# Capped attention and a spatial gating unit on one core: outputs issued by ScalarE, denominators as 28 rows of 32, v in two loads, a new order

## The chip, the cores and the metric

The kernel runs on one core of a Trainium2 chip. The metric is the device time of one execution in microseconds (us); shown is the median of 3 runs. PE is TensorE, DVE is VectorE, ACT is ScalarE, POOL is GpSimd, SP is SyncE, which in this kernel before the change issues every DMA.

## The reference

```python
# q, k, v: (8, 12, 448, 64)
scores = cap * tanh(q @ k.T / 8 / cap)
scores = scores - max(scores, axis=-1)
attn = exp(scores)
attn = attn / (sum(attn, axis=-1) + 1e-9)
x = (attn @ v)                      # heads put side by side: (8, 448, 768)
h = maximum(x @ w_in, 0)            # (8, 448, 1024), halves u and v
v_n = (v - mean(v)) / sqrt(var(v) + 1e-6)
v_s = w_spatial @ v_n + b_spatial   # over the 448 positions
out = (u * v_s) @ w_out             # (8, 448, 768)
```

cap is 30, w_in and w_out arrive as 64-bit floats.

## The kernel before

**Attention.** The 12 heads of a batch are worked in 3 quads of four heads, 24 quads in all (`quad_bnd`, called once per quad; `turn` counts them). Scores are computed transposed, keys on partitions: for each of the 7 blocks of 64 keys, four float32 products of 64 x 64 x 448 fill one PSUM tile of 128 x 896 (L584, task `sc`). ACT takes tanh (L588) and, for two blocks at a time, exp (L595). PE multiplies the exponentials by v (L605, task `pv`). Since the cap bounds the scores, exp is taken without subtracting the maximum; DVE finds the maximum of the exponentials (the reference's epsilon is scaled by it) and their sum by folding the tiles on each other (L623), a 32 x 32 block transpose (L631) and a reduction (L633), which leaves 28 columns for each of two partition halves. For the first three quads (`PE_SUMS = 3`) PE computes the sums with a matrix of ones (L651), ACT copies them out (L660), and they go through DRAM twice to get into the layout of the maxima: `td<-u` (L664), then `dt<-td` (L667).

**Denominators.** In `dt`, partition i holds one of 32 positions and the 28 columns the blocks of 32 queries, so positions lie block by block down the columns. DVE makes the denominator (L673) and its reciprocal (L675). Two DMAs write it to DRAM (`rd<-dt`, L676), two more spread it over the partitions of each head (`rr<-rd`, L680). DVE multiplies the attention output by it (L690, task `xmul`); rr is read there with a step of 14 elements. ACT and DVE then split the product into two parts whose sum carries float32 (L345 `xg<-xf`, L341 `xg<-xf`).

**The second part** (`moe`, once per batch; here "the FF block"): products with w_in (L743 to L745 for u, L765 to L770 for v), layer norm on DVE, ACT and POOL, products with w_spatial (L834 to L839), the gate (L844), products with w_out (L859 to L861), six copies out of PSUM per batch by ACT (L345 `o<-ps_acc`) and six stores by SP (L865, `out<-o`). Each product is three one-pass products of split operands. The weights are split at the start (L403 to L417, L341, L345).

**Order.** Every instruction is a task with an engine, an assumed length, a key and dependences. `Plan.order` simulates the engines with these lengths and takes, among the tasks that can start, the one with the smallest key; the keys come from the tables `BND_KEY`, `BND_ADJ`, `BND_W_KEYS`. Each engine, and SP's DMA queue, then works its list in that order. PE changes between its two ways of tiling (64-row products of attention, 128-row products of the FF block) when the list changes over; `STICK` is the planner's reluctance to do so. xg has 7 buffers, o 2, PSUM has two tiles each for `s` and `acc` and one for `x`.

```python
add("S", HW, k, lambda o=o, ns=ns: nc.sync.dma_start(out=out[b, ns, :], in_=o.t), [r], [o], lat=XF * 128 * S)
x, r = x.rearrange("p (b i) -> p b i", i=32), r.rearrange("p (i b) -> p b i", b=QB)
```

Of the kernel before, what the change touches and what calls it, by code (L numbers as in the profile page):

```python
# [9 lines left out]
F32 = mybir.dt.float32  # L10
# [32 lines left out]
class Plan:  # L43
# [8 lines left out]
    TURN, STICK = 180.0, 2.7208  # L52
# [31 lines left out]
    def order(self):  # L84
# [35 lines left out]
        while done < len(self.tasks):  # L120
# [24 lines left out]
            while again:  # L145
                again = False
                for e in ["A", *("VP" if holder == "V" else "PV"), "S", "T"]:
# [20 lines left out]
                    if e == "S":  # L168
                        dma = max(dma, took.end + 650.0) + took.lat
                        took.lat = dma + 1000.0 - took.end  # L170
# [13 lines left out]
HW, HH, XL, XF = 475, 650, 50, 4 / 360  # L184
# [24 lines left out]
def gpc(n):  # L209
# [21 lines left out]
    "v": (4 * D, F32, 4), "tp": (2 * PW, F32, 6),  # L231
    "xf": (PW, F32, 2), "rr": (PW, F32, 2), "st": (64, F32, 2), **MOE_TAGS, "xg": (XW, F32R, 7),
# [6 lines left out]
BND_KEY = dict(ld=15.1316, vld=10.6595, sc=-4.3972, th=0.8221, ex=-13.3346, pv=2.8747, sm=5.6221, mx=2.7207,  # L239
               dn=-3.5316, ev=-2.5342, x=1.255, moe=3.3159, span=11.7552, step=-1.2625, mv=-7.4324, vld_=0.4935, sc_=0.475,  # L240
               th_=0.213, ex_=2.8729, pv_=0.0973, sm_=0.5533, mx_=0.887)
BND_ADJ = dict(sc0=1.8257, sc1=1.698, sc2=0.6056, sc3=3.487, sc4=2.4891, sc5=0.9848, sc6=1.9465, sc7=1.2566,
               sc8=-0.2027, sc9=-0.0525, sc10=-1.0199, sc11=-1.6861, sc21=0.372, sc22=0.2759, sc23=-0.0304, mx0=4.147, mx1=2.3102,
               mx2=-1.5569, mx3=-2.5816, mx4=-1.7021, mx5=-3.8682, mx6=-3.7708, mx7=-2.1194, mx8=2.2658, mx9=6.0412, mx10=4.2055,
               mx11=1.3621, mx21=-0.5191, mx22=-1.2175, mx23=5.0057, sm0=1.8357, sm1=-4.3389, sm2=0.1127, sm3=-1.9888,
               sm4=-3.2252, sm5=-6.4566, sm6=-4.1062, sm7=-2.4598, sm8=-0.1718, sm9=4.6664, sm10=2.3463, sm11=0.4051,
               sm21=-1.2777, sm22=-3.1044, sm23=2.1372, dn0=-6.9641, dn1=1.8515, dn2=-0.9662, dn3=3.7809, dn4=8.6087, dn5=5.0673,
               dn6=1.1656, dn7=-2.366, dn8=0.4341, dn9=2.5001, dn10=4.9471, dn11=-4.3505, dn21=14.2648, dn22=10.8391, dn23=8.4438,
               x0=-1.2869, x1=-4.0561, x2=-5.6099, x3=-5.4773, x4=2.351, x5=0.6484, x6=4.0904, x7=0.1021, x8=2.4533, x9=6.1666,
               x10=4.3613, x11=1.3018, x21=-0.0656, x22=-3.6008, x23=0.1225, moe0=-0.4749, moe1=-0.3715, moe2=-0.6357,  # L250
               moe3=-0.003, moe7=-4.8205, span0=0.237, span1=0.5291, span2=-5.1693, span3=-3.6031, span7=51.1417, mv0=3.2517,
               mv1=1.1849, mv2=5.0071, mv3=5.7847, mv7=-5.1134, wi0=-11.8899, wi1=-7.682, wi2=-25.3033, wi3=9.6125, wi4=12.6292,
               wi5=4.2564, wi6=0.1225, wi7=-1.8938, wi8=-6.6204, wi9=0.3494, wi10=-1.8774, wi11=-9.6153, ws0=-12.9749, ws1=4.598,
               ws2=-15.4035, ws3=-9.2649, wo0=-5.5216, wo1=-4.7934, wo2=-5.3784, wo3=1.0364)
# [12 lines left out]
def attn_moe(ctx, tc, bounded, shared, qk, v, qk2, v2, cap, w_in, w_sp, w_out, out):  # L267
# [95 lines left out]
    def split_f32(key, c):  # L363
# [27 lines left out]
    def split_f64(key, src, hi, lo, n, late=False):  # L391
# [11 lines left out]
        t = add("S", HW, key, lambda: nc.sync.dma_start(out=w.t.bitcast(U32)[:, :2 * n], in_=src), allocs=[w], lat=XF * 256 * n)  # L403
# [39 lines left out]
    def v_any(b, hp, key):  # L443
# [3 lines left out]
        a = add("S", HW, key - 1, lambda: nc.sync.dma_start(out=r.t, in_=v[b, hp]), allocs=[r], lat=XF * 128 * 512)  # L447
# [4 lines left out]
    def head_any(b, h, vt, vdep, xf, rr, after):  # L452
# [9 lines left out]
        t0 = add("S", 2 * HW, k - 2.0, ld, allocs=[raw], lat=XF * 128 * 896)  # L462
# [42 lines left out]
        def den():  # L505
# [8 lines left out]
                   [rr] if e == 0 else [], lat=XF * D * S)  # L514
# [40 lines left out]
    def quad_bnd(b, n):  # L555
# [5 lines left out]
        for c in range(2):  # L561
# [15 lines left out]
        for i in range(NB):
# [39 lines left out]
        sec = lambda i: dt.t[:96, i * n1:(i + 1) * n1]  # L617
        done = []
        for a, op, key in ((0, ALU.max, "mx"), (1, ALU.add, "sm"))[:1 if by_pe else 2]:
            r = Buf("red")  # L620

            def fold(o_, i0, i1, op=op):
# [11 lines left out]
                out=st.t[:, a * n1:(a + 1) * n1], in_=blk(r1()), axis=AX.X), [d, *done], [r, st], [st] if a == 0 else [], name="red3"))  # L634
        d = done
        for c in range(2):
            p = slice(2 * c * 32, (2 * c + 1) * 32)
            o = slice((2 * c + 1) * 32, (2 * c + 2) * 32)
            d = [add("A", 145, kk("dn"), lambda p=p, o=o: nc.scalar.copy(out=sh.t[p, :n1 * len(done)], in_=st.t[o, :n1 * len(done)]), d,
                     [st, sh], [sh] if c == 0 else [], name="shift")]  # L640
        d = add("V", 106, kk("dn"), lambda: nc.vector.tensor_tensor(sec(0), st.t[:96, :n1], sh.t[:96, :n1], op=ALU.max), d,
                [st, sh, dt], [dt], name="mred2")
        if by_pe:
            accs, sxs, td = [Buf("acc"), Buf("acc")], [Buf("u"), Buf("u")], Buf("td")
# [14 lines left out]
            for c in range(2):  # L659
                q = add("A", act(S) + 420, kk("ev"), lambda c=c: nc.scalar.copy(  # L660
                    out=sxs[c].t.rearrange("p (i b) -> p b i", b=QB), in_=accs[c].t[:, 0, :S].rearrange("p (b i) -> p b i", i=32)), [s],
                    [accs[c], sxs[c]], [sxs[c]], name="sev")
                for e in range(2):
                    outs.append(add("S", HW, kk("dn"), lambda c=c, e=e: nc.sync.dma_start(  # L664
                        out=td.t[(2 * c + e) * S:(2 * c + e + 1) * S], in_=sxs[c].t[D * e:D * e + 1]), [q], [sxs[c], td],
                        [] if outs else [td], lat=XL))
            d1 = [d] + [add("S", HW, kk("dn"), lambda c=c: nc.sync.dma_start(  # L667
                out=dt.t[2 * c * 32:(2 * c + 1) * 32, 2 * n1:3 * n1].rearrange("p (e b) -> p e b", b=QB),
                in_=td.t[2 * c * S:2 * (c + 1) * S].rearrange("(e p b) -> p e b", e=2, b=QB)), [d, *outs], [td, dt], lat=XL) for c in range(2)]
        else:  # L670
            d1 = [add("V", 106, kk("dn"), lambda: nc.vector.tensor_tensor(sec(1), st.t[:96, n1:2 * n1], sh.t[:96, n1:2 * n1], op=ALU.add), [d],
# [272 lines left out]
```

## Time and profile before

| | |
|---|---|
| median of 3 runs | 735.85 us (735.57 to 736.28) |
| the profiled execution | 735.29 us |
| its span, first to last instruction | 733.5 us |
| mean granted clock of TensorE | 0.994 of full |
| PE busy | 716.0 us (98%) |
| DVE busy | 609.6 us (83%) |
| ACT busy | 481.4 us (66%) |
| POOL busy | 79.0 us (11%) |
| DMA | 66.52 MB, mean 91 GB/s |

A busy row of PE is the union of its matmuls, whose ends are modelled, so it holds both work and slow stretches. The row of a line tells how many instructions it had, the busy time of all, the mean of one in ns, and the idle time of the engine just before them with what ended it.

### The profile page before, as it was taken

How to read it: one execution, taken by the hardware profiler on the slowest of the kernel's cores; microseconds unless marked ns; L12 is line 12 of the kernel's file. 1: busy time of each engine (PE TensorE's matmuls, PEld its weight loads, DVE VectorE, ACT ScalarE, POOL GpSimd, SP SyncE). 2: the span in 40 equal slices, each digit the busy share in tenths (PEclk: the TensorE clock that was granted, in tenths of full speed). 3: DMA queues.
4: the chain of work that ended last, by engine and by line, in shares of the span. 5: the costliest groups of instructions: out<-in, count | busy, mean ns of one | idle time of the engine just before them, and what ended most of it. 6: DMA issues, size and time to landing. Idle time of an engine off the chain costs nothing.

```text
span 733.5 us, 12340 instructions
## 1 busy us (share of the span) xinstructions
PE 716.0 (98%) x4902; PEld 485.3 (66%) x4902; DVE 609.6 (83%) x825; ACT 481.4 (66%) x648; POOL 79.0 (11%) x69
## 2 busy tenths in 40 slices
PE   8997999999999999999999999999999999999997
PEld 2333675574587586955778557767659576679896
DVE  4999999999999998949999299989899598884620
ACT  6999865858856957388573794867773865833421
POOL 1353011500100002000210003000020001000100
PEclk9998999999999999999999999999999999999999
DMA  7556232533212432052230431214311321002002
GB/s 268 192 192 200 67 111 63 164 102 107 90 32 85 143 100 76 1 150 82 72 102 11 140 103 33 69 44 160 101 47 56 101 76 51 26 26 88 14 2 80
DMA packets 43167, 66.52 MB, mean 91 GB/s; under 512 B 8782, under 2 KB 33884, under 8 KB 43100
## 3 DMA queue, kind: packets, MB, share of 16 engines
q1 hardware_dynamic: 43100, 65.64, 28.3%
q8 instruction: 40, 0.66, 0.4%
q14 instruction: 27, 0.22, 0.1%
HBM read 54.42 MB, written 11.20 MB: 89 GB/s over the span
## 4 chain that ended last, share of the span: by engine, by line
PE 63%; DVE 21%; ACT 6%; DMA 5%; issue 3%; SPq 1%; POOL 0%; DVEq 0%; ACTq 0%
PE ps_s L584 10%; PE ps_x L605 9%; DVE red L623 8%; PE ps_acc L859 4%; PE ps_acc L860 4%; PE ps_acc L861 4%; PE ps_acc L743 4%; PE ps_acc L744 4%; PE ps_acc L745 4%; DMA rr<-rd 3%; PE ps_acc L768 2%; PE ps_acc L770 2%; PE ps_acc L769 2%; ACT tp L595 2%; PE ps_acc L837 2%
## 5 line engine op out<-in xcount | busy, mean ns | idle before, releaser
L588 ACT ACTIVATE tp<-ps_s,capt 128x896 f32<-128x896 f32 x168 | 162.3, 1005 | 19.7 <-PE ps_s L584 13.7
L595 ACT ACTIVATE tp<-tp,capt 128x1792 f32<-128x1792 f32 x96 | 154.3, 1609 | 1.5
L623 DVE TENSOR_TENSOR red<-red,tp 128x1792 f32<-128x1792 f32 x90 | 140.0, 1555 | 14.7 <-ACT tp L595 13.2
L584 PE MATMUL ps_s<-raw 64*64 64x448 f32 x1344 | 147.1, 544 | 3.0 <-ACT tp L588 2.7
L605 PE MATMUL ps_x<-tp,v 64*64 64x448 f32 x1344 | 140.6, 537 | 2.0 <-ACT tp L595 1.7
L623 DVE TENSOR_TENSOR red<-tp 128x1792 f32<-128x1792 f32 x45 | 90.9, 2021 | 24.1 <-ACT tp L595 23.1
L605 PEld LDWEIGHTS ps_x<-tp,v 64*64 64x64 f32 x1344 | 50.4, 133 | 78.2 <-issue 67.8
L584 PEld LDWEIGHTS ps_s<-raw 64*64 64x64 f32 x1344 | 46.2, 132 | 80.4 <-issue 43.8
L792 POOL TENSOR_TENSOR lst<-lst,capt 128x1 f32<-128x1 f32 x32 | 38.6, 1208 | 521.8 <-DVE lst L790 521.8
L743 PE MATMUL ps_acc<-xg,wi_h 128*128 128x448 f32 x180 | 67.7, 376 | 3.2 <-ACT xg L345 3.2
L744 PE MATMUL ps_acc<-xg,wi_h 128*128 128x448 f32 x180 | 66.1, 367 | 1.2 <-DVE xg L341 1.2
L745 PE MATMUL ps_acc<-xg,wi_l 128*128 128x448 f32 x180 | 66.1, 367 | 0.0
L859 PE MATMUL ps_acc<-xg,wo_h 128*128 128x448 f32 x176 | 65.2, 371 | 0.4 <-DVE o L844 0.3
L860 PE MATMUL ps_acc<-xg,wo_h 128*128 128x448 f32 x176 | 64.0, 364 | 0.5 <-DVE xg L341 0.5
L861 PE MATMUL ps_acc<-xg,wo_l 128*128 128x448 f32 x176 | 63.6, 361 | 0.0
L690 DVE TENSOR_TENSOR xf<-xf,rr 128x448 f32<-128x448 f32 x48 | 44.4, 951 | 20.8 <-DMA rr<-rd 20.8
L345 ACT CAST xg<-o 128x448 fp32r<-128x448 f32 x32 | 17.9, 566 | 61.5 <-DVE o L844 53.5
L623 DVE TENSOR_TENSOR red<-red 128x896 f32<-128x896 f32 x45 | 50.6, 1123 | 0.5
L631 DVE STREAM_TRANSPOSE red<-red 128x896 f32<-128x896 f32 x45 | 49.6, 1103 | 0.5
L768 PE MATMUL ps_acc<-wi_h,xg 128*128 128x512 f32 x126 | 50.0, 397 | 0.0
L633 DVE TENSOR_REDUCE st<-red 128x28 f32<-128x896 f32 x45 | 48.6, 1079 | 0.8
L769 PE MATMUL ps_acc<-wi_l,xg 128*128 128x512 f32 x126 | 49.1, 390 | 0.0
(141 smaller groups left out, 1121.0 us busy)
## 6 DMA issues: line engine op xcount, KB each, us to landing
raw<-in_qk SPq DMA_DIRECT2D x48, 448.0 KB
rr<-rd SPq DMA_DIRECT2D x48, 224.0 KB
out<-o SPq DMA_DIRECT2D x48, 224.0 KB
v<-in_v SPq DMA_DIRECT2D x72, 128.0 KB
w<-in_w_in SPq DMA_DIRECT2D x12, 512.0 KB
xg<-in_w_out SPq DMA_DIRECT2D x12, 256.0 KB
v<-in_v SPq DMA_DIRECT2D x24, 64.0 KB
rd<-dt SPq DMA_DIRECT2D x48, 3.5 KB
```

The source lines that it names most:

```text
L584: nc.tensor.matmul(ps.t[c * D:(c + 1) * D, e, :S], lhsT=f(raw[c].t)[r, k:k + D], rhs=f(raw[c].t)[r, :S], start=True, stop=True)
L588: th = add("A", act(PW, 1), kk("th", i), lambda ps=ps, tp=tp, o=o: nc.scalar.activation(out=tp.t[:, o:o + PW].rearrange("p (e q) -> p e q" ...
L595: ex = add("A", act_s(w, 1), kk("ex", i), lambda tp=tp, w=w: nc.scalar.activation(out=tp.t[:, :w], in_=tp.t[:, :w], func=AF.Exp, scale=ca) ...
L605: nc.tensor.matmul(x.t[e * D:(e + 1) * D, c, :S], lhsT=vts[g].t[c * D:(c + 1) * D, (2 * j + e) * D:(2 * j + e + 1) * D], rhs=tp.t[c * D:(c ...
L623: nc.vector.tensor_tensor(o_(), i0(), i1(), op=op)
L743: nc.tensor.matmul(ps, lhsT=wi1_h[:, c, fs], rhs=x[:, XH:], start=(c == 0), stop=False)
L744: nc.tensor.matmul(ps, lhsT=wi1_h[:, c, fs], rhs=x[:, :S], start=False, stop=False)
L745: nc.tensor.matmul(ps, lhsT=wi1_l[:, c, fs], rhs=x[:, XH:], start=False, stop=(c == NP - 1))
L768: nc.tensor.matmul(ps, lhsT=x[:, XH:][:, ts], rhs=wi2_h[:, c], start=(c == 0), stop=False)
L859: nc.tensor.matmul(ps, lhsT=wo_h[:, c, ns], rhs=g[:, XH:], start=(c == 0), stop=False)
L860: nc.tensor.matmul(ps, lhsT=wo_h[:, c, ns], rhs=g[:, :S], start=False, stop=False)
L861: nc.tensor.matmul(ps, lhsT=wo_l[:, c, ns], rhs=g[:, XH:], start=False, stop=(c == 3))
```

## The change

- The six stores of a batch are issued by ACT (`nc.scalar.dma_start`), right behind the copies in ACT's own list, in place of SP.
- Maxima and sums stay in `st` in sections of 32 columns, of which 28 are used. A block transpose on DVE (task `dtr`, one per quad) turns them into 28 rows of 32, so that a row holds 32 queries that follow each other. `rd<-dt` moves 28 rows of 32 elements in place of 32 x 2 runs of 14, and rr comes out in the order of xf: the multiply reads both without a step.
- The sums of the first three quads are copied out of PSUM without a rearrangement and go straight from `u` into `dt` by DMA; the trip through `td` is gone.
- v of a quad is loaded in two pieces (128 x 512 and 128 x 384) into two buffers, in place of four pieces into four; the memory is the same.
- The planner's assumed lengths for DMAs change, and all keys are new, so the order of all engines is new.

```diff
-            add("S", HW, k, lambda o=o, ns=ns: nc.sync.dma_start(out=out[b, ns, :], in_=o.t), [r], [o], lat=XF * 128 * S)
+            add("A", 340, kv(k), lambda o=o, ns=ns: nc.scalar.dma_start(out=out[b, ns, :], in_=o.t), [r], [o], lat=2500, name="odma")
...
-    "v": (4 * D, F32, 4), "tp": (2 * PW, F32, 6),
-    "xf": (PW, F32, 2), "rr": (PW, F32, 2), "st": (64, F32, 2), **MOE_TAGS, "xg": (XW, F32R, 7),
+    "v": (8 * D, F32, 2), "tp": (2 * PW, F32, 6),
+    "xf": (PW, F32, 2), "rr": (PW, F32, 2), **MOE_TAGS, "xg": (XW, F32R, 7),
...
-        for g in range(4):
-            w = min(4 * D, PW - 4 * D * g)
+        for g in range(2):
+            w = min(8 * D, PW - 8 * D * g)
...
-                q = add("A", act(S) + 420, kk("ev"), lambda c=c: nc.scalar.copy(
-                    out=sxs[c].t.rearrange("p (i b) -> p b i", b=QB), in_=accs[c].t[:, 0, :S].rearrange("p (b i) -> p b i", i=32)), [s],
+                q = add("A", act(S), kk("ev"), lambda c=c: nc.scalar.copy(out=sxs[c].t, in_=accs[c].t[:, 0, :S]), [s],
                     [accs[c], sxs[c]], [sxs[c]], name="sev")
                 for e in range(2):
                     outs.append(add("S", HW, kk("dn"), lambda c=c, e=e: nc.sync.dma_start(
-                        out=td.t[(2 * c + e) * S:(2 * c + e + 1) * S], in_=sxs[c].t[D * e:D * e + 1]), [q], [sxs[c], td],
-                        [] if outs else [td], lat=XL))
-            d1 = [d] + [add("S", HW, kk("dn"), lambda c=c: nc.sync.dma_start(
-                out=dt.t[2 * c * 32:(2 * c + 1) * 32, 2 * n1:3 * n1].rearrange("p (e b) -> p e b", b=QB),
-                in_=td.t[2 * c * S:2 * (c + 1) * S].rearrange("(e p b) -> p e b", e=2, b=QB)), [d, *outs], [td, dt], lat=XL) for c in range(2)]
+                        out=dt.t[64 * c + e * QB:64 * c + (e + 1) * QB, 32:64],
+                        in_=sxs[c].t[D * e:D * e + 1].rearrange("p (b i) -> p b i", i=32)), [q, room], [sxs[c], dt], lat=dm(QB, 128)))
+            d = [add("V", 106, kk("dn"), lambda: nc.vector.transpose(out=sec(dt, 0), in_=sec(st, 0)), [d, room], [st, dt], name="dtr"), *outs]
...
+            d = [add("V", 140, kk("dn"), lambda: nc.vector.transpose(out=dt.t[:96, :64].rearrange("p (a i) -> p a i", i=32),
+                in_=st.t[:96, :64].rearrange("p (a i) -> p a i", i=32)), [d, room], [st, dt], name="dtr")]
...
-            out=rd.t[2 * c * S:2 * (c + 1) * S].rearrange("(e p b) -> p e b", e=2, b=QB),
-            in_=dt.t[2 * c * 32:(2 * c + 1) * 32, :n1].rearrange("p (e b) -> p e b", b=QB)), [d], [dt, rd], [] if c else [rd], lat=XL)
+            out=rd.t[c * PW:(c + 1) * PW].rearrange("(p i) -> p i", i=32), in_=dt.t[64 * c:64 * c + n1, 32:64]), [d], [dt, rd], [] if c else [rd],
+            lat=dm(n1, 128)) for c in range(2)]
...
-                x, r = x.rearrange("p (b i) -> p b i", i=32), r.rearrange("p (i b) -> p b i", b=QB)
                 eng[E_X[0]].tensor_tensor(x, x, r, op=ALU.mult)
...
-BND_KEY = dict(ld=15.1316, vld=10.6595, sc=-4.3972, th=0.8221, ex=-13.3346, pv=2.8747, sm=5.6221, mx=2.7207,
+BND_KEY = dict(ld=21.3368, vld=21.4975, sc=-5.2844, th=0.946, ex=-11.0691, pv=4.9062, sm=6.2433, mx=2.4129,
```

What the new keys do to the lists is shown at three places; in the new kernel lines L584, L743, L690, L341, L345 and L865 are L592, L749, L696, L349, L353 and L871.

PE's list at the first products of the FF block, before (`raw` is q and k, `xg` the split attention output, `wi_h` and `wi_l` the parts of w_in):

```order
L584 MATMUL ps_s<-raw_158 64x448 x2
L743 MATMUL ps_acc<-xg,wi_h 128x448
L744 MATMUL ps_acc<-xg,wi_h 128x448
L745 MATMUL ps_acc<-xg,wi_l 128x448
L743 MATMUL ps_acc<-xg,wi_h 128x448
L744 MATMUL ps_acc<-xg,wi_h 128x448
L745 MATMUL ps_acc<-xg,wi_l 128x448
L584 MATMUL ps_s<-raw_157 64x448 x2
L584 MATMUL ps_s<-raw_158 64x448 x2
L584 MATMUL ps_s<-raw_157 64x448 x2
L584 MATMUL ps_s<-raw_158 64x448 x2
L743 MATMUL ps_acc<-xg,wi_h 128x448
```

And now:

```order
L592 MATMUL ps_s<-raw_61 64x448 x2
L749 MATMUL ps_acc<-xg,wi_h 128x448
L750 MATMUL ps_acc<-xg,wi_h 128x448
L751 MATMUL ps_acc<-xg,wi_l 128x448
L749 MATMUL ps_acc<-xg,wi_h 128x448
L750 MATMUL ps_acc<-xg,wi_h 128x448
L751 MATMUL ps_acc<-xg,wi_l 128x448
L592 MATMUL ps_s<-raw_60 64x448 x2
L592 MATMUL ps_s<-raw_61 64x448 x2
L749 MATMUL ps_acc<-xg,wi_h 128x448
```

Ahead of the first six products stand 68 groups of four 64-row products before and 71 now; between them and the next products stand two groups before and one now.

DVE's list at the same place (`xf<-xf,rr` is the multiply by the reciprocal, `xg<-xf,xg` the second part of the split, `wy` and `wi_l` the splitting of w_in), before:

```order
L690 TENSOR_TENSOR xf<-xf,rr 128x448 x2
L341 TENSOR_TENSOR wi_l<-wy,wi_h 128x512
L341 TENSOR_TENSOR xg<-xf,xg 128x448 x3
L641 TENSOR_TENSOR dt_172<-st,sh_164 96x28
L414 TENSOR_SCALAR wy<-wy 128x512
```

And now:

```order
L696 TENSOR_TENSOR xf<-xf,rr 128x448 x2
L422 TENSOR_SCALAR wy<-wy 128x512 x2
L349 TENSOR_TENSOR xg<-xf,xg 128x448 x2
L423 SCALAR_TENSOR_TENSOR wy<-w_649,wy 128x512
L349 TENSOR_TENSOR xg<-xf,xg 128x448
L425 SCALAR_TENSOR_TENSOR wy<-w_649,wy 128x512
L349 TENSOR_TENSOR xg<-xf,xg 128x448
L650 TENSOR_TENSOR st_165<-st_165,sh_161 96x28
```

Before, one of the four splits of the first two quads stands earlier in the list, behind the first quad's multiply, and three stand here; now all four stand here, behind the second quad's multiply.

ACT's list at the first stores, before (`o<-ps_acc` is the copy out of PSUM, `tp<-ps_s` tanh, `tp<-tp` exp):

```order
L345 COPY o<-ps_acc 128x448 x3
L588 ACTIVATE tp<-ps_s,capt 128x896 x2
L345 COPY o<-ps_acc 128x448
L595 ACTIVATE tp<-tp,capt 128x1792
L345 COPY o<-ps_acc 128x448
```

And now:

```order
L353 COPY o<-ps_acc 128x448
L871 DMA out<-o 128x448
L353 COPY o<-ps_acc 128x448
L871 DMA out<-o 128x448
L353 COPY o<-ps_acc 128x448
L871 DMA out<-o 128x448
L596 ACTIVATE tp<-ps_s,capt 128x896 x2
L353 COPY o<-ps_acc 128x448
L603 ACTIVATE tp<-tp,capt 128x1792
L871 DMA out<-o 128x448
```

Each copy now has its store behind it in ACT's list; of the 48 stores 26 have another copy of this kind next, and 4 have a tanh next.

## Rows read from the trace of the kernel before

**Rows 1.** The page's busy times and slices of PE, and the granted clock.

```profile
PE 716.0 (98%) x4902; PEld 485.3 (66%) x4902; DVE 609.6 (83%) x825; ACT 481.4 (66%) x648; POOL 79.0 (11%) x69
...
PE   8997999999999999999999999999999999999997
...
PEclk9998999999999999999999999999999999999999
```

**Rows 2.** What PE waited for: us in total, times, longest.

```profile
PE ps_acc L743 <- ACT xg L345: 3.2, 1, 3.2
PE ps_s L584 <- ACT tp L588: 2.7, 7, 0.7
PE ps_x L605 <- ACT tp L595: 1.7, 3, 0.8
...
PE ps_acc L744 <- DVE xg L341: 1.2, 1, 1.2
PE ps_acc L651 <- POOL wy L410: 0.9, 1, 0.9
PE ps_acc L860 <- DVE xg L341: 0.5, 1, 0.5
PE ps_x L605 <- ACT xf L611: 0.3, 1, 0.3
PE ps_acc L859 <- DVE o L844: 0.3, 1, 0.3
```

**Rows 3.** The chain that ended last, 60 to 75 us: start, us, what.

```profile
60.64 1.49 DMA rd<-dt
...
62.82 5.15 DMA rr<-rd
...
67.99 1.77 DVE xf L690 x2
...
70.36 1.52 DVE xg L341 x2
```

**Rows 4.** Timeline of PE, 55 to 80 us: start, us, line, count, idle before.

```profile
65.00 1.85 PE L584 MATMUL ps_s<-raw 64*64 64x448 f32 x16
70.03 0.74 PE L743 MATMUL ps_acc<-xg,wi_h 128*128 128x448 f32 x1 [3.18 <-ACT xg L345]
71.93 0.74 PE L744 MATMUL ps_acc<-xg,wi_h 128*128 128x448 f32 x1 [1.16 <-DVE xg L341]
```

**Rows 5.** Windows: PE, PEld, DVE, ACT, POOL busy, PEclk, DMA share, GB/s.

```profile
65.00:70.00 5.00, 1.85 (x17) 0.41 (x16) 4.04 (x5) 4.06 (x6) 1.15 (x2) 0.96 0.88 232
70.00:75.00 5.00, 3.81 (x9) 3.08 (x10) 5.00 (x8) 4.92 (x10) 0.95 (x1) 0.50 0.33 120
75.00:80.00 5.00, 5.00 (x38) 3.15 (x41) 5.00 (x8) 3.74 (x5) 0.00 (x0) 0.86 0.08 10
```

**Rows 6.** Groups by form: busy us, mean ns, idle before and its releasers.

```profile
L690 DVE TENSOR_TENSOR xf<-xf,rr 128x448 f32<-128x448 f32 x48 | 44.4, 951 | 20.8 <-DMA rr<-rd 20.8
L341 DVE TENSOR_TENSOR xg<-xf,xg 128x448 fp32r<-128x448 f32 x48 | 28.9, 631 | 3.5 <-ACT xg L345 3.5
...
L641 DVE TENSOR_TENSOR dt<-st,sh 96x28 f32<-96x28 f32 x24 | 4.2, 179 | 2.7 <-ACT sh L639 2.6
```

**Rows 7.** Groups by form: the copies of ACT.

```profile
L345 ACT COPY o<-ps_acc 128x448 f32<-128x448 f32 x44 | 23.5, 535 | 30.0 <-PE ps_acc L861 25.9 <-DVE red L623 2.1 <-ACT xg L345 1.0
...
L660 ACT COPY u<-ps_acc 128x448 f32<-128x448 f32 x6 | 5.2, 984 | 0.0
```

**Rows 8.** Line L865 on SP's queue: ns min/median/max, first and last start.

```profile
L865 SPq DMA_DIRECT2D out<-o x48: 332/338/585, 155.0 to 729.0; - x48
```

**Rows 9.** What SP's queue waited for: us in total, times, longest.

```profile
SPq L865 <- ACT o L345: 92.6, 33, 36.8
SPq L865 <- ACT sh L639: 54.8, 4, 24.0
```

**Rows 10.** Timeline of the last 8.5 us, the last copy out of PSUM.

```profile
728.41 0.53 ACT L345 COPY o<-ps_x 128x448 f32<-128x448 f32 x1 [1.87 <-PE ps_x L861]
```

More of the change, by code (lines that the diff above doesn't have):

```diff
@@ L169, in order @@
                         dma = max(dma, took.end + 650.0) + took.lat
-                        took.lat = dma + 1000.0 - took.end
+                        took.lat = dma + 900.0 + 0.55 * took.lat - took.end
                     busy[e] = took.end
@@ L183, with dm @@
 FF = 751
-HW, HH, XL, XF = 475, 650, 50, 4 / 360
+HW, HH, XL = 400, 620, 50
+def dm(packets, size):
+    return packets * (4.0 + 0.0016 * size)
 def act(n, extra=0):
@@ L633, in quad_bnd @@
             done.append(add("V", dve(PW), kk(key, 5), lambda r1=r1, a=a, red=red: red(
-                out=st.t[:, a * n1:(a + 1) * n1], in_=blk(r1()), axis=AX.X), [d, *done], [r, st], [st] if a == 0 else [], name="red3"))
+                out=st.t[:, a * 32:a * 32 + n1], in_=blk(r1()), axis=AX.X), [d, *done], [r, st], [st] if a == 0 else [], name="red3"))
         d = done
@@ L638, in quad_bnd @@
             o = slice((2 * c + 1) * 32, (2 * c + 2) * 32)
-            d = [add("A", 145, kk("dn"), lambda p=p, o=o: nc.scalar.copy(out=sh.t[p, :n1 * len(done)], in_=st.t[o, :n1 * len(done)]), d,
+            d = [add("A", 145, kk("dn"), lambda p=p, o=o: nc.scalar.copy(out=sh.t[p, :32 * len(done)], in_=st.t[o, :32 * len(done)]), d,
                      [st, sh], [sh] if c == 0 else [], name="shift")]
-        d = add("V", 106, kk("dn"), lambda: nc.vector.tensor_tensor(sec(0), st.t[:96, :n1], sh.t[:96, :n1], op=ALU.max), d,
-                [st, sh, dt], [dt], name="mred2")
+        room = add("S", 0, kk("dn"), lambda: None, [done[0]], [dt], [dt])
+        d = add("V", 106, kk("dn"), lambda: nc.vector.tensor_tensor(sec(st, 0, n1), sec(st, 0, n1), sec(sh, 0, n1), op=ALU.max), d,
+                [st, sh], name="mred2")
         if by_pe:
-            accs, sxs, td = [Buf("acc"), Buf("acc")], [Buf("u"), Buf("u")], Buf("td")
+            accs, sxs = [Buf("acc"), Buf("acc")], [Buf("u"), Buf("u")]
             def ones(g):
@@ L682, in quad_bnd @@
             in_=rd.t.rearrange("(c e q) -> c e q", c=2, e=2)[:, e].unsqueeze(0).broadcast_to([D, 2, S])), d, [rd, rr],
-            [] if e else [rr], lat=XF * D * PW) for e in range(2)]
+            [] if e else [rr], lat=dm(128, 4 * S)) for e in range(2)]
         deps = out + [z]
```

76 lines of the change are left out of this document (38 added, 38 removed).

## The prediction

> **What bounds the kernel now.** I read the page first: PE is busy 716.0 of 733.5 us, DVE 83%, ACT 66%, and in the slices of the span PE falls below nine tenths only at the two ends and in slice 4, where the granted clock dips as well [rows 1]. So the kernel is bound by PE, and a part of the change counts only where it shortens PE's work or takes away time in which PE stands or runs slowly. The reader should look for that time next: the table of PE's waits. It is short. One place holds most of it, the first products of the FF block, with 3.2 us on ACT's split and 1.2 us on DVE's; all other waits come to 2.7 + 1.7 + 0.9 + 0.5 + 0.3 + 0.3 = 6.4 us [rows 2].
>
> The timeline shows that place: PE is through with its scores at 66.85, starts one product at 70.03, the next at 71.93 [rows 4]. The windows show what the gap costs beyond itself: the granted clock is 1.00 up to there, then 0.96, 0.50 and 0.86 in three stretches of 5 us [rows 5], that is 0.2 + 2.5 + 0.7 = 3.4 us of full-speed time, at the lower of the two levels (1.2 GHz) from about 70 to 76. The gap and the dip together are 4.3 + 3.4 = 7.7 us, the largest single loss behind the start. The chain says what ended last there: the second quad's reciprocal goes out (1.49 us) and comes back (5.15 us), then two multiplies (1.77 us), then splits [rows 3].
>
> **The change, part by part,** against the profiled execution's 735.29 us. The median shown is 0.56 us above it.
>
> *Matrix work.* By the lists PE has the same products before and after: 357 groups of four 64-row products, 2032 products of the FF block, and 61 turns between the two kinds. Term 0.
>
> *The first products.* Ahead of them PE now has three more groups, of about 0.75 us each (16 records, two groups, fill the 1.5 us steps of such runs; 1.85 us with the tail of the last [rows 4]), but the first split is no longer ready early: all four splits of the first two quads stand behind the second quad's multiply. Before, PE had run six products of 0.2 us ahead of the gap, and two groups after them. So PE arrives with about 1.1 us less done, 65.8 in place of 66.85. The chain that it waits for gets shorter: the trip through `td` is gone and two multiplies lose 0.32 us each [rows 6]. By counting DVE's list with its own means, the second quad's reciprocal stands 1.7 us of work earlier. The first split is then done near 69.2 in place of 70.9 for the one that PE waited for, and the fourth near 71.8 in place of 72.4. What PE has behind it at 72 is 0.8 us more than now. The clock dips as before, since PE still stands about as long in one piece as it did (3.2 us). Term -0.8; ends -7.7 (gap and dip gone) and +4.1 (below).
>
> *DVE.* The multiply reads without a step: from 951 to 631 ns, the row of the same shape that has none [rows 6], 48 times: -15.4 us. Added are 24 small transposes; no row has that shape, the small operations beside it take 179 ns [rows 6], so I take 24 x 0.18 = 4.3 us (the end above is the 1.1 us of the large transpose, 26 us, which I drop for its size of 896 columns). DVE gains about 11 us, but PE's waits on DVE outside the first products are 0.5 + 0.3 us [rows 2]. Term -0.4; ends -0.8 and 0. What hides the rest is PE's own work; if DVE were to lose time, its wait on rr of 20.8 us would be the first to show [rows 6].
>
> *Stores on ACT.* No row shows ACT issuing a DMA. The nearest is the same store on SP, 332 to 585 ns, median 338 [rows 8]: 48 x 0.338 = 16.2 us on ACT, ends 15.9 and 28.1. Behind a store on ACT wait the next copy, split or tanh. The copies have room: ACT idles 25.9 us ahead of 44 of them, for PE [rows 7], 0.6 us each, and 26 of 48 stores have another copy behind them. What can reach PE is a store with a tanh behind it, 4 of them: at most 4 x 0.585 = 2.3 us, at least 0. I take half of 4 x 0.338: +0.7. The copies of PE's sums lose 984 - 535 = 449 ns, six times [rows 7], which is inside the term on the first products, where ACT has little idle time (4.06 of 5 us busy, then 4.92 [rows 5]).
>
> *SP's queue.* The stores no longer make SP wait; two of those waits alone are 92.6 + 54.8 us [rows 9], and q, k, v and rr loads stand behind them. But PE's table has no wait for a DMA [rows 2]. Term 0; ends -0.5 and 0. Here the price in transfers is also 0, since the bytes are the same.
>
> *v in two loads.* The first piece is twice as large: 128 KB more at 232 GB/s [rows 5] is 0.6 us later at the start, where ACT paces PE. Term +0.1; ends 0 and +0.6. Later the second half of a buffer comes free later, but v is needed a whole quad after.
>
> *The rest of the order.* The waits that are left, mostly on ACT, are 5.6 us [rows 2]. With new keys they can all go, or as much can appear elsewhere: ends -5.6 and +5.6. By the lists attention ends earlier against the FF block: 424 of the 2032 products stand behind the last 64-row group in place of 366, so tanh and exp of the last quads have more cover. I take -1.6.
>
> *The end.* The last copy ends at 728.94 [rows 10] and its store is issued at 729.0; on ACT the hop to SP goes. Term -0.1; ends -0.1 and +0.25 (the spread of rows 8).
>
> Sum: -0.8 - 0.4 + 0.7 + 0 + 0.1 - 1.6 - 0.1 = -2.1, so 733.2 in a profiled execution, and with the 0.56 us **733.7 us** as a median.
>
> **The rivals.** A difference below 0.2% (1.5 us) can't be told from none here.
>
> *The gap and the dip go* (727). The terms besides the first one are -1.3; with -7.7 in its place the time is 735.85 - 9.0 = 726.9. For it: the chain is shorter at three steps. Against: the return of rr, 5.15 us, is not changed, and the four splits would have to be done by 66, 5 us earlier than now.
>
> *The gap grows* (739, slower). Now all products of the FF block hang on the second quad's multiply. If it starts at 68.0 as before, its two multiplies (1.3 us), then a piece of the weights' splitting and the splits follow, and the first is done near 70.8: PE stands 5.0 us in one piece in place of 4.3 in two, so 0.7 us more, and a second stretch at the low level as long as the first costs 3.4: 735.85 - 1.3 + 4.1 = 738.7. It decides if that multiply starts later than about 67. For it: DMA share is 0.88 in just this stretch [rows 5], so rr can take longer; before, one split was ready early. Against: the reciprocal stands earlier in the list.
>
> *Nothing that can be told* (735.9). PE's work and turns are the same, SP and DVE are covered, and ACT's stores eat what the order gives. For it stand the 98% [rows 1]. The Trainium skill, in DMA: Bandwidth & Descriptors (Issuing engines are not separate DMA queues), says that starting DMAs from several engines saves only the sequencer's time to start them; by that rule the ACT queue gives no faster transfers, and the trace agrees in so far as PE has 0 us of DMA waits.
>
> *A new gap elsewhere* as large as this one, from the new keys: 735.85 - 2.1 + 7.7 = 741.5.
>
> **How the numbers follow.** Forecast 0.43, no difference 0.20, gap grows 0.17, gap goes 0.14, new gap 0.06. The forecast's own range is 731.5 to 736, of which 0.30 lies below 734.4 (faster), 0.12 within 1.5 us and 0.01 above. Faster: 0.30 + 0.14 + 0.03 of the others = 0.47; same: 0.12 + 0.15 = 0.27; slower: 0.15 + 0.06 + 0.05 = 0.26. The range from 727.5 to 739.5 leaves out most of the case at 727, the one at 741 and the outer part of the case at 739, less than 0.2 together.
>
> **What would show it.** Right: PE busy still 97 to 98%; PE's wait at the first product near 3.4 us and the clock low for some 6 us behind it; multiplies at 0.62 to 0.65 us; stores on ACT at 0.33 to 0.6 us; ACT busy nearly unchanged, since issues are not counted. Wrong: a PE wait over 2 us anywhere behind 100 us, a wait on a DMA of v or rr in PE's table, or stores on ACT above 1 us, with tanh late behind them. If the clock stays at full speed through 60 to 80 us, the first rival holds.

## The result: 0.9% slower, and the profile after

The changed kernel takes 742.1 us (median of 5 runs, 740.21 to 742.99) against 735.84 us; the ratio is 1.0094, with an interval from 1.0074 to 1.0113. The profiled execution took 742.99 us, its span 741.2 us, 7.7 us more than the span before.

The page's busy row and slices of PE, which answer to [rows 1]:

```profile
PE 724.5 (98%) x4902; PEld 486.7 (66%) x4902; DVE 603.2 (81%) x849; ACT 480.2 (65%) x648; POOL 63.5 (9%) x71
...
PE   8988999999999999999999999999999999999997
...
PEclk9988999999999999999999999999999999999999
```

PE has the same 4902 products and is busy 8.5 us longer. Slices 3 and 4 dip now, PE and clock, where before it was slice 4 alone. The table of PE's waits, against [rows 2] (us in total, times, longest):

```profile
PE ps_s L592 <- ACT tp L596: 4.3, 6, 2.3
PE ps_x L613 <- ACT tp L603: 3.6, 3, 3.2
...
PE ps_acc L660 <- ACT tp L603: 0.9, 1, 0.9
PE ps_acc L749 <- ACT xg L353: 0.9, 1, 0.9
PE ps_acc L866 <- DVE xg L349: 0.3, 1, 0.3
PE ps_acc L750 <- DVE xg L349: 0.3, 1, 0.3
```

The wait of 3.2 us at the first products is down to 0.9 us, but waits of 3.2 us on an exp and of 2.3 us on a tanh are new. The sum is 10.3 us, against 10.8 before, so waits alone do not make the difference. The timeline of PE says where they are, against [rows 4], and the windows what the clock does there, against [rows 5]:

```profile
50.61 3.26 PE L613 MATMUL ps_x<-tp,v 64*64 64x448 f32 x16 [3.18 <-ACT tp L603]
...
70.44 3.27 PE L592 MATMUL ps_s<-raw 64*64 64x448 f32 x16 [2.35 <-ACT tp L596]
74.60 0.47 PE L749 MATMUL ps_acc<-xg,wi_h 128*128 128x448 f32 x1 [0.89 <-ACT xg L353]
```

```profile
50.00:55.00 5.00, 4.39 (x24) 1.54 (x28) 5.00 (x9) 4.70 (x8) 1.75 (x3) 0.50 0.17 64
55.00:60.00 5.00, 5.00 (x48) 1.79 (x44) 2.80 (x9) 3.77 (x5) 0.00 (x0) 0.84 0.49 136
...
70.00:75.00 5.00, 3.66 (x17) 0.87 (x17) 3.79 (x7) 4.97 (x9) 0.69 (x1) 0.66 0.68 218
75.00:80.00 5.00, 3.96 (x16) 2.00 (x16) 4.87 (x12) 4.90 (x11) 0.00 (x0) 0.71 0.21 71
```

So there are two gaps, each with a stretch at the lower clock behind it. The first has a chain behind it that the timelines of SP's queue, DVE and ACT show, one fence each:

```profile
31.76 1.81 SPq L672 DMA_DIRECT2D dt<-u  x2
...
34.24 1.58 SPq L672 DMA_DIRECT2D dt<-u  x2
```

```profile
37.90 0.19 DVE L681 SCALAR_TENSOR_TENSOR dt<-dt 96x32 f32<-96x32 f32 x1 [2.39 <-DMA dt<-u]
...
44.51 0.39 DVE L380 CAST ws_h<-wy 128x448 fp32r<-128x448 f32 x1 [0.68 <-DMA wy<-in_w_sp]
...
47.54 0.68 DVE L425 SCALAR_TENSOR_TENSOR wy<-w,wy 128x512 uint32<-128x512 uint32 x1
```

```profile
48.25 0.62 ACT L353 CAST wi_h<-wy 128x512 fp32r<-128x512 f32 x1 [2.98 <-DVE wy L425]
48.77 1.78 ACT L603 ACTIVATE tp<-tp,capt 128x1792 f32<-128x1792 f32 x1
```

DVE waits for the sums' DMA and for a piece of w_spatial, 3.07 us together; a cast of w_in on ACT waits 2.98 us for DVE; the exp behind that cast waits with it, and PE waits 3.18 us for the exp.

The gaps do not explain all of it: before had one too. The groups by form show a second loss (busy us, mean ns of one). The kernel before, then the changed one:

```profile
L745 PE MATMUL ps_acc<-xg,wi_l 128*128 128x448 f32 x180 | 66.1, 367 | 0.0
L861 PE MATMUL ps_acc<-xg,wo_l 128*128 128x448 f32 x176 | 63.6, 361 | 0.0
L769 PE MATMUL ps_acc<-wi_l,xg 128*128 128x512 f32 x126 | 49.1, 390 | 0.0
L838 PE MATMUL ps_acc<-ws_l,vh 128*128 128x448 f32 x87 | 31.4, 361 | 0.0
```

```profile
L751 PE MATMUL ps_acc<-xg,wi_l 128*128 128x448 f32 x180 | 65.9, 366 | 0.0
L867 PE MATMUL ps_acc<-xg,wo_l 128*128 128x448 f32 x176 | 64.3, 366 | 0.0
L775 PE MATMUL ps_acc<-wi_l,xg 128*128 128x512 f32 x126 | 49.7, 394 | 0.0
L844 PE MATMUL ps_acc<-ws_l,vh 128*128 128x448 f32 x87 | 31.9, 366 | 0.0
...
L696 DVE TENSOR_TENSOR xf<-xf,rr 128x448 f32<-128x448 f32 x48 | 28.4, 617 | 3.5 <-DMA rr<-rd 2.4 <-ACT xf L619 1.0
...
L679 DVE STREAM_TRANSPOSE dt<-st 96x64 f32<-96x64 f32 x21 | 4.9, 236 | 0.2
```

In these rows, in which no product waits, one takes 4 to 5 ns more with w_out, with w_in at 512 columns and with w_spatial. Four or five ns look like nothing in a row, but the FF block has 2032 products. Records of products that follow each other overlap, so look at the time from start to start as well: in the timelines behind 85 us, where products of one kind follow each other (some 1900 of the 2032), its mean rises from 200 to 204 ns with w_in at 448 columns and with w_out, from 227 to 233 at 512 columns and from 201 to 203 with w_spatial. So w_in at 448 columns is slower too, though its row does not show it (367 and 366). Over these products the difference comes to 7 us.

One thing that the change did beside its purpose could do this: st moved from a pool into two constant tiles, sh and dt changed their widths, and everything allocated behind them moved. The parts of the half of w_in that makes u and those of w_out (wi1, wo) lie 576 bytes further on, xg, vh and vl 128 bytes earlier. The other half of w_in, of the 512-column products, and w_spatial lie ahead of st and stay where they were.

### The profile page after: what moved, and what is told of

It is laid out like the page before. It is cut to its first block, busy times and chain, and to the rows that moved or that the text cites. A ratio compares the mean times of both kernels' runs of the same rounds, so it can differ in the third digit from the quotient of the medians.

```text
span 741.2 us, 12250 instructions
## 1 busy us (share of the span) xinstructions
PE 724.5 (98%) x4902; PEld 486.7 (66%) x4902; DVE 603.2 (81%) x849; ACT 480.2 (65%) x648; POOL 63.5 (9%) x71
## 4 chain that ended last, share of the span: by engine, by line
PE 83%; DVE 6%; ACT 6%; DMA 2%; issue 2%; POOL 1%; SPq 0%; POOLq 0%; DVEq 0%; ACTq 0%
PE ps_s L592 14%; PE ps_x L613 13%; PE ps_acc L749 5%; PE ps_acc L750 5%; PE ps_acc L751 5%; PE ps_acc L865 4%; PE ps_acc L774 4%; PE ps_acc L866 4%; PE ps_acc L867 4%; PE ps_acc L776 4%; PE ps_acc L775 4%; DVE red L631 2%; ACT tp L596 2%; PE ps_acc L843 2%; PE ps_acc L844 2%; PE ps_acc L845 2%
## 5 line engine op out<-in xcount | busy, mean ns | idle before, releaser
L592 PE MATMUL ps_s<-raw 64*64 64x448 f32 x1344 | 149.4, 550 | 4.7 <-ACT tp L596 4.3
L592 PEld LDWEIGHTS ps_s<-raw 64*64 64x64 f32 x1344 | 46.9, 134 | 82.3 <-issue 42.3
L798 POOL TENSOR_TENSOR lst<-lst,capt 128x1 f32<-128x1 f32 x32 | 29.3, 915 | 542.0 <-DVE lst L796 533.0
L749 PE MATMUL ps_acc<-xg,wi_h 128*128 128x448 f32 x180 | 67.2, 373 | 0.9 <-ACT xg L353 0.9
L865 PE MATMUL ps_acc<-xg,wo_h 128*128 128x448 f32 x176 | 65.3, 371 | 0.0
L774 PE MATMUL ps_acc<-wi_h,xg 128*128 128x512 f32 x126 | 50.6, 402 | 0.0
L776 PE MATMUL ps_acc<-wi_h,xg 128*128 128x512 f32 x126 | 49.8, 395 | 0.0
L631 DVE TENSOR_TENSOR red<-red 128x896 f32<-128x896 f32 x45 | 48.6, 1080 | 0.5
L353 ACT CAST xg<-o 128x448 fp32r<-128x448 f32 x32 | 18.1, 566 | 47.1 <-DVE o L850 43.1
```

The costliest lines, as they stand in the source:

```text
L592: nc.tensor.matmul(ps.t[c * D:(c + 1) * D, e, :S], lhsT=f(raw[c].t)[r, k:k + D], rhs=f(raw[c].t)[r, :S], start=True, stop=True)
L631: nc.vector.tensor_tensor(o_(), i0(), i1(), op=op)
L749: nc.tensor.matmul(ps, lhsT=wi1_h[:, c, fs], rhs=x[:, XH:], start=(c == 0), stop=False)
L774: nc.tensor.matmul(ps, lhsT=x[:, XH:][:, ts], rhs=wi2_h[:, c], start=(c == 0), stop=False)
L865: nc.tensor.matmul(ps, lhsT=wo_h[:, c, ns], rhs=g[:, XH:], start=(c == 0), stop=False)
```

## The experiments

**Old keys with the new parts, new keys with the old parts.**

```diff
-    TURN, STICK = 180.0, 5.007
+    TURN, STICK = 180.0, 2.7208
...
-BND_KEY = dict(ld=21.3368, vld=21.4975, sc=-5.2844, th=0.946, ex=-11.0691, pv=4.9062, sm=6.2433, mx=2.4129,
+BND_KEY = dict(ld=15.1316, vld=10.6595, sc=-4.3972, th=0.8221, ex=-13.3346, pv=2.8747, sm=5.6221, mx=2.7207,
```

> The changed kernel with the keys, the reluctance and the DMA lengths of the planner as they were before. Theory of the order (the new lists make a second gap near 47 us and a slow stretch behind it): that gap is gone, PE's largest wait is at the first products of the FF block again, and the time is 733 to 737 us. Theory of the placement (the moved tiles make each 512-column product slower, 402 against 397 ns in its row): that mean stays at 401 or more and the time is at least 738. Theory of ACT's queue (stores issued there disturb PE or ACT): at least 739, since ACT still issues them.

Measured: 750.2 us, ratio 1.0179 (1.016 to 1.0199). PE's waits:

```profile
PE ps_acc L865 <- DVE o L850: 4.5, 2, 4.2
PE ps_x L613 <- ACT tp L603: 3.1, 1, 3.1
```

The reverse edit, in the kernel before:

> The kernel before with the new keys, the new reluctance and the new DMA lengths; stores on SP, v in four loads and the trip through td stay. Theory of the order: 739 to 744 us, with a PE wait of over 2 us on ACT's exp or tanh ahead of 68 us. Theories of the placement and of ACT's queue: 733 to 737 us, with a mean of the 512-column products of w_in near 397 ns.

Measured: 778.44 us, 1.0584 (1.0565 to 1.0603).

```profile
PE ps_s L589 <- ACT tp L593: 20.5, 15, 7.6
```

Both times missed. With the other tasks each set of keys makes lists with large gaps of their own, so these two runs do not part the order from the rest. They say one thing, in the rows of the 512-column products with w_in's lower part, first of the new parts with the old keys, then of the reverse:

```profile
L775 PE MATMUL ps_acc<-wi_l,xg 128*128 128x512 f32 x126 | 49.7, 395 | 0.0
```

```profile
L774 PE MATMUL ps_acc<-wi_l,xg 128*128 128x512 f32 x126 | 49.1, 390 | 0.0
```

The slow products go with the new parts, not with the new order. (The expectations name the row of the upper part, `wi_h,xg`: 397 ns before and 402 in the changed kernel, 400 and 397 in these two runs.)

**Stores on SP again**, each at the place in the global order where ACT issues it.

```diff
-nc.scalar.dma_start(out=out[b, ns, :], in_=o.t), [r], [o], lat=2500
+nc.sync.dma_start(out=out[b, ns, :], in_=o.t), [r], [o], lat=2500
```

> The changed kernel with its stores issued by SP again, at the place in the global order at which ACT issues them, so that the other engines' lists stay. Theory of ACT's queue: 3 to 7 us less, 735 to 739 us. Theory of the order: within 1.5 us of the changed kernel, 740.5 to 743.5, or slower where SP's loads stand behind a store that waits.

Measured: 742.68 us (739.79 to 744.78), 1.0082 (1.0063 to 1.0101), the row with w_in's lower part at 394 ns. Who issues the stores changes neither the time, within the spread, nor the products. The Trainium skill, in DMA: Bandwidth & Descriptors (Issuing engines are not separate DMA queues), says that DMAs run on the same 16 engines whichever engine starts them, and that starting them from several saves only the sequencer's time to start them. The run agrees: 742.1 us with ACT and 742.68 with SP.

**The old addresses.** The lists are those of the changed kernel; st, sh1 and a few unused bytes are placed so that each operand of a matmul lies where it lay before (but for the matrix of ones, 64 bytes further on).

```diff
-        keep("sh", DEN, 64, 1.0)
-        keep("st", DEN, 64, 1.0)
+        keep("sh", 1, 64, 1.0)
+        const.tile([128, 48], F32, name="gap")
...
+        if g == "rr" and bounded:
+            sts = pool("sts", 1)
```

> The changed kernel with its constant tiles moved so that every operand of the matmuls lies at the address that it had before; the lists are the same. Theory of the placement: the 512-column products fall from 402 to 397 ns and the time by 4 to 6 us, to 736 to 738. Theories of the order and of ACT's queue: within 1 us of the changed kernel, 741 to 743 us, and the mean stays at 401 to 402 ns.

Measured: 734.54 us (732.19 to 736.58, 12 runs), 0.9983 (0.9969 to 0.9997).

```profile
L762 PE MATMUL ps_acc<-xg,wi_l 128*128 128x448 f32 x180 | 65.6, 364 | 0.0
L878 PE MATMUL ps_acc<-xg,wo_l 128*128 128x448 f32 x176 | 63.7, 362 | 0.0
L786 PE MATMUL ps_acc<-wi_l,xg 128*128 128x512 f32 x126 | 49.2, 390 | 0.0
...
L855 PE MATMUL ps_acc<-ws_l,vh 128*128 128x448 f32 x87 | 31.4, 360 | 0.0
```

The slow products are gone. With one row for each kind, 576 x 2 ns with w_in, 576 x 4 with w_out, 528 x 4 of 512 columns and 96 x 6 with w_spatial come to 6.1 us of the 8.2 us between the two profiled executions (742.99 and 734.82); since records overlap, this is an estimate. The gaps are not quite alike either: the granted clock in the windows of 5 us between 50 and 85 us falls to 0.66 twice here, where it falls to 0.50, 0.84, 0.66, 0.71 and 0.95 in the changed kernel, and PE waits 11.2 us here, 10.3 there. A cleaner price of the placement is that of the next run.

**The reverse: the kernel before with 128 unused bytes.**

```diff
+        const.tile([128, 16], F32, name="gap")
     wi1_h, wi1_l = weights("wi1", NP, FH)
...
+        if g == "xg" and bounded:
+            pool("gap", 1).tile([128, 16], F32, name="gap")
```

> The kernel before, with 64 unused bytes ahead of w_in's parts and 64 more ahead of xg: the same offsets against a multiple of 256 bytes as in the changed kernel, and nothing else changed. Theory of the placement: the 512-column products rise from 390 to 394 or 395 ns, those with w_out from 361 to 366, and the time by 5 to 8 us, to 739.5 to 743.5. If placement matters only together with the new lists: within 1 us of the kernel before.

Measured: 740.62 us (739.8 to 741.13), 1.0075 (1.0055 to 1.0094).

```profile
L868 PE MATMUL ps_acc<-xg,wo_l 128*128 128x448 f32 x176 | 64.3, 366 | 0.0
...
L776 PE MATMUL ps_acc<-wi_l,xg 128*128 128x512 f32 x126 | 49.7, 394 | 0.0
```

A kernel with the old parts and the old lists, and two unused tiles, is 0.75% slower, with the rows of the changed kernel. Its gap and its clock are those of the kernel before: the same waits of 3.2 and 1.2 us at the first products, and 0.97, 0.50 and 0.85 between 65 and 80 us, against 0.96, 0.50 and 0.86 [rows 5]. So 5.5 us (740.62 against 735.14 in runs of the kernel before beside it) are the placement alone. That settles the second loss.

**Which address.** Four more placements, each one unused tile ahead of xg (in b2 one more ahead of vh) or the old place of the weights:

```diff
+        if g == "xg" and bounded:
+            pool("gap", 1).tile([128, 32], F32, name="gap")
```

> The changed kernel with one unused tile of 128 bytes ahead of the xg tiles; the lists are the same, and w_in's and w_out's parts stay 576 bytes behind their old place. Theory A (what counts is where xg, vh and vl lie): the whole effect of the old addresses comes back, 733 to 736 us, with the 512-column products at 390 and the products with w_out at 362 to 368. Theory B (the parts of w_in and w_out count too): only part of it, 736 to 740 us; the 512-column products recover, the 448-column ones with w_in and w_out stay at 366. Theory C (neither, another tile): 740 to 743 us.

> As the run with 128 unused bytes ahead of xg, and 64 more ahead of vh, so that xg, vh, vl and all weights begin on a multiple of 256 bytes. If each operand off such a multiple costs time, the 448-column products with w_spatial gain 1 to 4 ns in 528, so 0.5 to 2 us less than without the 64 bytes; if only xg counts, within 0.5 us of it.

> The changed kernel with 192 unused bytes ahead of xg: against a multiple of 256 bytes xg begins at 64, the parts of w_in and w_out at 0, vh and vl at 0. Theory of the distance (a product is fast where the one operand lies 64 bytes past the other, as in the kernel before with xg at 0 and the weights at 192): products with w_in and w_out are fast again, 361 to 363 ns, those of 512 columns slow at 394 to 396, about 738 to 740 us. Theory of xg's own place (only 0 is fast): both slow, 741 to 744 us. Theory of the weights' own place (192 fast, 0 slow): products with w_out slow, 365 to 367.

> The changed kernel with w_in's and w_out's parts at their old addresses and 128 unused bytes ahead of xg: xg begins at 128, the weights at 192. Theory of the distance: it is 192 in place of 64 for the products with w_out, which no run has had alone; 361 to 363 ns if 64 and 192 are alike, 365 to 367 if not; those of 512 columns slow, 394 to 396. Theory of xg's own place: both slow, about 741 us. Theory of the weights' own place: products with w_out fast, 361 to 363.

Places are bytes past a multiple of 256; the three last columns are the mean ns of the rows of `wi_l,xg`, `xg,wo_l` and `ws_l,vh`. Each ratio is against the kernel before in runs beside that kernel's own (its medians lie between 734.36 and 735.97 us), so compare the ratios.

| kernel | xg | wi1, wo | vh, vl | us | ratio | 512 columns | w_out | w_spatial |
|---|---|---|---|---|---|---|---|---|
| before | 0 | 192 | 192 | 735.84 | 1 | 390 | 361 | 361 |
| changed, old addresses | 0 | 192 | 192 | 734.54 | 0.9983 | 390 | 362 | 360 |
| changed | 128 | 0 | 64 | 742.1 | 1.0094 | 394 | 366 | 366 |
| before, 128 unused bytes | 128 | 0 | 64 | 740.62 | 1.0075 | 394 | 366 | 366 |
| b1_gap128 | 0 | 0 | 192 | 737.59 | 1.0045 | 390 | 366 | 361 |
| b2_gap128_64 | 0 | 0 | 0 | 739.66 | 1.0067 | 390 | 366 | 367 |
| d1_gap192 | 64 | 0 | 0 | 739.99 | 1.0062 | 396 | 361 | 366 |
| d2_old_gap128 | 128 | 192 | 64 | 740.0 | 1.0056 | 394 | 364 | 364 |

The rows of d1, in which the two kinds go opposite ways:

```profile
L780 PE MATMUL ps_acc<-wi_l,xg 128*128 128x512 f32 x126 | 49.8, 396 | 0.0
...
L872 PE MATMUL ps_acc<-xg,wo_l 128*128 128x448 f32 x176 | 63.5, 361 | 0.0
```

b1 came out as its theory B, d1 as the theory of the distance. With w_out xg streams and the weights are loaded: fast where xg lies 64 bytes past them (0 and 192, 64 and 0), slow at a distance of 0 or 128, and between the two at 192 (d2, 364 ns, which neither expectation had). Neither operand has a good place of its own, since xg at 0 is fast beside weights at 192 and slow beside weights at 0. The products with w_spatial have 448 columns too, with the weights (at 0 in all kernels) streaming and vh loaded, and go the same way: fast with vh at 192, which is again a distance of 64. From start to start, taken as in the section on the result, all products of 448 columns take 200 to 201 ns at a distance of 64, 202 to 203 at 192, and 203 to 206 at 0 and 128. At 512 columns the other half of w_in (at 0 in all kernels) streams and xg is loaded: fast with xg at 0 (227 ns from start to start), slow at 64 and 128 (233). Since these weights never moved, no run says whether the distance or xg's own place counts there. And more alignment is no help: with vh on a multiple of 256 too, the products with w_spatial rise, against both expectations of b2, and the time is 739.66 us, against 737.59 (the intervals of the two ratios, 1.005 to 1.0084 and 1.0027 to 1.0064, overlap). First b1, then b2:

```profile
L849 PE MATMUL ps_acc<-ws_l,vh 128*128 128x448 f32 x87 | 31.4, 361 | 0.0
```

```profile
L851 PE MATMUL ps_acc<-ws_l,vh 128*128 128x448 f32 x87 | 31.9, 367 | 0.0
```

The Trainium skill, in TensorE: Matmul & The Clock Gate (Step-by-step: what each phase is for), says that streaming and weight loading have a read port each, so that loading the next weights takes nothing from the running product. The weight loads themselves last the same (187 to 188 ns with w_out in both kernels), but the products differ by up to 6 ns with the place of one operand against the other; the measurement decides. That it is the loads that slow the stream is not shown.

**Seven xg tiles at four places in one kernel.**

> The changed kernel with its seven xg tiles at four places against a multiple of 256 bytes: xga 0 (two tiles), xgb 64 (two), xgc 128 (two), xgd 192 (one). Theory of the multiple: products that read xga are the fastest (448 columns at 360 to 363 ns, 512 at 389 to 390), those with the three others are all 3 to 5 ns slower. Theory of another bound (multiples of 128): xga and xgc alike. Theory of one bad place: only xgc slow. Time 737 to 742 us in the first case.

Measured: 741.46 us, one run. None of the three theories holds: at 512 columns xga, at 0, takes 391 ns in place of 390, xgb and xgc 394 to 396, and with w_out the rows lie between 363 and 372. Products follow each other on different tiles here, so each row mixes distances. It tells nothing beyond that.

**The gap in front.** First the exp ahead of the cast that it stands behind (on top of b1):

```diff
+            tasks[i], tasks[i + 1] = tasks[i + 1], tasks[i]
```

> As the run with 128 unused bytes ahead of xg, and in ACT's list the exp of the second quad stands ahead of the cast of w_in that waits there for DVE (2.98 us in the changed kernel), one pair exchanged. Theory of the order in front: PE's wait of 2.8 to 3.2 us on that exp goes, and with it the slow clock of 50 to 55 us; 2 to 5 us less than without the exchange. Rival (ACT stays the bound between 40 and 80 us, so that the wait comes back at 68 to 75 us): within 1 us of it.

Measured: 738.16 us, 1.0052 (1.0032 to 1.0071), where b1 has 1.0045. The time is the rival's, the reason is not, since the wait comes back at once and not at 68 to 75 us:

```profile
PE ps_acc L665 <- ACT u L674: 2.8, 1, 2.8
```

ACT is held at the same place by the same late DVE, and the next thing that PE needs from it, the copy out of a PSUM tile, is as late as the exp was. The slow stretch can't be read from this pair: between 50 and 60 us the granted clock is 1.00 in b1, behind a wait of 3.0 us, and 0.87 and 0.78 here, behind one of 2.8 us. So a gap of this size does not always have a dip behind it. The wait must go from DVE. At the old addresses, the denominator behind the next fold, alone and then with the cast of w_spatial two instructions later:

```diff
+            i = next(i for i, t in enumerate(tasks) if t.name == "den")
+            j = next(i for i, t in enumerate(tasks) if t.name == "rec")
+            behind(i, j - 1)
+            behind(150, 156)
```

> As the changed kernel at the old addresses, with the denominator alone moved behind the fold. If the sums' DMA alone made DVE late: PE's wait on the exp falls below 0.8 us, 731 to 733 us. If the load of w_spatial would have held DVE anyway: DVE's wait on that load grows from 0.6 to 2.5 us or more, PE's wait stays above 2 us, and the time within 1 us of 734.5.

Measured: 738.01 us (734.96 to 739.26), 1.0036 (1.0019 to 1.0052).

```profile
ACT wi_h L364 <- DVE wy L436: 3.2, 1, 3.2
...
DVE ws_h L391 <- DMA wy<-in_w_sp: 1.7, 1, 1.7
```

The wait on the sums is gone and the one on w_spatial has grown from 0.6 to 1.7 us; ACT still waits, and PE waits 3.4 us for the exp, where it waited 2.8. Neither expectation met the time: it is 3.5 us above the old addresses alone. In the windows the granted clock is lower for longer, 0.51 and 0.81 between 50 and 60 us in place of 0.66 and 1.00, and 0.66, 0.74 and 0.92 between 70 and 85 us in place of 1.00, 0.66 and 1.00. Why the dips are longer is left open.

> The changed kernel at the old addresses, and in DVE's list two waits taken away: the first quad's denominator behind the fold that follows it (it waited 2.39 us for the sums' DMA), the cast of a piece of w_spatial two instructions later (0.68 us for its load). Theory of the chain in front (these waits make DVE late, DVE makes ACT's cast of w_in wait 2.6 to 3.0 us, and the exp behind it makes PE wait 2.8 to 3.2 us): PE's wait on that exp falls below 0.5 us, and the time by 2 to 4 us against the old addresses alone, to 730.5 to 732.5. Rival (PE then waits for ACT at 65 to 75 us for as much longer): PE's wait there grows from 2.3 to 4 us or more and the time stays within 1 us of 734.5.

Measured: 731.4 us (729.63 to 734.03, 12 runs), 0.9955 (0.9938 to 0.9971): faster than both kernels. By the ratios that is 2.1 us less than the old addresses alone; the two intervals touch. The wait of 2.8 us on the exp that the old addresses alone still have is gone, and the clock is at 1.00 from 40 to 70 us:

```profile
PE ps_s L603 <- ACT tp L607: 4.4, 6, 2.5
...
PE ps_x L624 <- ACT tp L614: 0.8, 3, 0.3
```

The longest wait on a tanh, at 66 us, is 2.5 us where it was 2.3, so the rival fails.

> As the run with the two DVE instructions later, and the third quad's copies of PE's sums behind the tanh that PE waits 2.3 us for, and a piece of w_in behind the second quad's multiply on DVE. Theory: that tanh starts 0.84 us earlier, PE's wait there falls to about 1.5 us and the time by 0.5 to 1.5 us more. Rival (the first split sets the end of the gap, not the tanh): PE waits as much longer for the split, time within 0.5 us of the run without it.

Measured: 732.84 us, 0.9967 (0.9953 to 0.9981). The wait on that tanh falls from 2.46 to 1.59 us, as expected, but the next on a tanh grows by as much, from 0.43 to 1.30, and nothing is gained; the time is 1.4 us higher, with overlapping intervals. It is not quite the rival either: the wait grows on a tanh, not on the split (1.76 us before, 1.32 now). ACT is busy all through this stretch (4.97 of 5 us in each window from 60 to 70 us).

## Why the prediction was wrong

**The step that failed is the first: "Matrix work. Term 0".** I counted products and turns, and the counts were right. That the same product costs the same was taken for granted. It does not: the change moves the operands in memory, and the products of the FF block cost 5.5 us more where nothing else is changed (740.62 against 735.14), 6 to 8 us by the rows and the start-to-start times of the changed kernel. No rival had it, so the range ended at 739.5. Nor do the signs of being wrong that I had named show it: no wait over 2 us behind 100 us, no wait of PE on a DMA, stores at 338 to 390 ns. Without it (old addresses) the change is at 0.9983, 1.3 us faster than before; I had said 2.1. That this is so near is in part luck: at the old addresses PE waits 2.5 us at the first products, where it waited 4.4, and 8.7 us elsewhere, where it waited 6.4.

**The first products (-0.8).** Right: PE's wait there, 3.18 and 1.16 us before, is 0.89 and 0.26 now, and the trip through DRAM is gone. Wrong: I took the shorter path as a gain only. The new transfer out of one partition costs SP a median of 778 ns to issue, twelve times, in place of 242 ns, and DVE waits 2.39 us for it. That wait, with 0.68 us for w_spatial, comes out as PE's gap at 47 us, with its own slow stretch. How much of DVE's wait is the price of the issue, and how much the sums' copies, which ACT ends at 32.8 in place of 31.3 us, no run separates. This gap is the rival of a new gap elsewhere, to which I gave 0.06, at a place before the first products. That its 741.5 us lies beside the measured 742.1 is luck: it had 7.7 us for the gap, and taking this gap away at the old addresses gained 2 to 3 us. Everything behind it is late: the second quad's multiplies start at 71.54, where they started at 67.99 [rows 3] and I had counted on less. In front of them PE now waits for a tanh, since ACT has no idle time there.

**DVE (-0.4).** The multiply takes 617 ns, where I had 631; the transposes 236 ns in place of 180. DVE is 6.4 us less busy, where I had counted 11, and PE's waits on DVE outside the first products fall from 0.8 to 0.3 us, near the term.

**Stores on ACT (+0.7).** 338 to 390 ns, median 338, as taken. The measured term is 0 within the spread: 742.1 us with ACT and 742.68 with SP. A wait that I had not named is there and is covered: ACT's copies wait 19.1 us, ten times, for earlier stores to land and free o.

**SP's queue and v (0, +0.1).** PE waits for neither.

**The rest of the order (-1.6).** Behind 80 us PE waited 1.7 + 0.5 + 0.3 + 0.3 = 2.8 us before, and 0.8 + 0.3 + 0.2 = 1.3 us now. There the term was right. But it stood for all waits outside the first products, 6.4 us before, and these are 4.3 + 3.6 + 0.9 + 0.3 = 9.1 us now: ahead of 80 us they grew from 3.6 to 7.8 us, by the gap above and the tanh at 70 us. The term had the wrong sign.

## What to carry to other kernels

An edit that adds, widens or moves a tile moves everything allocated behind it; where PE is the bound, compare the mean of one product in the rows of both kernels before looking for waits, and put the operands back with unused bytes before judging the edit. When an engine's wait goes and the time stays, look one instruction further down the same queue: here two waits of DVE had to go together, and moving the instruction that suffered changed only who suffered.

## What the runs showed of the hardware that I had not expected

- The time of a product depends on where its two operands begin relative to each other: 361 ns and 366 ns with w_out, 390 and 394 to 396 at 512 columns, with weight loads unchanged at 188 ns. The 448-column products are fastest with the streamed operand 64 bytes past the loaded one (counted within multiples of 256), the 512-column ones with xg at 0, the only one of three places tried. Why is left open.
- A DMA of 14 rows of 32 elements out of a single partition into SBUF holds its queue for 737 to 972 ns; the same bytes as one row to DRAM took 214 to 403 ns.
